# Float32r matmuls that read their moving tile from the last column to the first, in a long-convolution and feed-forward kernel

## Chip, core and metric

The kernel runs on one core of one Trainium2 chip. The metric is the device time of one execution in microseconds. Before the change it is 3116.07 us, the median of 3 runs (3114.22 to 3117.28).

## What is computed

For 4 sequences of 12480 positions and 128 channels, a filter is made from position embeddings by a small two-layer network and a decaying window, `x * v` is convolved with it along the sequence, and the result is multiplied by `x`. Each of the 49920 rows then goes through a feed-forward layer of width 2048 with a squared ReLU:

```python
u = x * v
y = irfft(rfft(u, 2 * S, axis=1) * rfft(h_filt, 2 * S, axis=0), 2 * S, axis=1)[:, :S]
x = (x * y).reshape(B * S, D)
h = np.maximum(x @ w_in, 0.0)
out = h * h @ w_out
```

## The kernel before

The convolution is a transform in four stages for each of the four sequences (`stage1` to `stage4`, lines 232 to 677). The stages are matmuls with tables of sines and cosines, and between them all values stay in the tile `W` in SBUF. Stage one to three use float32 matmuls. Stage four (`mm`, line 570) splits its operands in a high and a low word, `ah` and `al`, and multiplies them as float32r: for each of 56 values of `t` it calls `mm3` twice. `mm3` (lines 92 to 97) issues three matmuls into one accumulator: high weights by high moving words, low weights by high moving words, high weights by low moving words. Each of the three has its own 112 columns of weights and streams 256 columns. `out_t` (line 603) multiplies the accumulator by `x`, transposes and stores the rows to `zd` in DRAM. For the first sequence, `turn_first` (line 581) does the same for the first two values of `t` and feeds the first feed-forward tile directly.

The feed-forward takes 98 tiles of tokens (2 of 446, 50 of 512, 46 of 510 columns; `GN`, line 32), and each tile in 8 steps, 784 steps in all. In a step `m_h` (line 785) issues 2 x 3 matmuls of `zh` and `zl` against 128 x 128 weights into `A`; `m_g` and `m_l` square the ReLU of `A` and split it into `gh` and `gl`, on ScalarE and VectorE, element by element and in the same column order; `m_o` (line 823) issues 2 x 3 matmuls of `gh` and `gl` into the output accumulator, which collects all 8 steps of a tile. All of these are `mm3`. That makes 784 x 12 = 9408 float32r matmuls in the feed-forward, and 224 x 6 = 1344 in stage four. A third user of `mm3`, in the filter network, has 42.

The order of the work on each engine is written out by hand: the loop at line 871 runs the feed-forward steps, and `adv` (line 850) interleaves pieces of the transforms of sequences one to three. So the tensor engine gets matmuls of the feed-forward and of the stages alternately, until the transforms are done. From then on (the tail, from about 2650 us) only the feed-forward is left, and the tiles of every second step come from a pool of their own, `tp`, opened at line 878; all other feed-forward tiles come from `mp`.

```python
def mm3(o, L, R, first=True, last=True):
    lh, ll = L
    rh, rl = R
    nc.tensor.matmul(o, lh, rh, start=first, stop=False)
    nc.tensor.matmul(o, ll, rh, start=False, stop=False)
    nc.tensor.matmul(o, lh, rl, start=False, stop=last)
```

Of the kernel before, what the change touches and what calls it, by code (L numbers as in the profile page):

```python
# [7 lines left out]
F32 = mybir.dt.float32  # L8
# [9 lines left out]
I = 112  # L18
# [9 lines left out]
NS = NF // 2  # L28
# [10 lines left out]
TH = 4  # L39
CW = 256  # L40
NCW = DFF // CW


@with_exitstack
def hyena_moe_kernel(
# [34 lines left out]
    def pool(name, side="left", **kw):  # L80
        return tc.tile_pool(name=name, bufs=kw.pop("bufs", 2), side=side, reuse_waits="tile", **kw)

    def bank():
        return psf.tile([128, 512], F32, tag="F", name="F")

    def idle(k):

        o = pso.tile([128, 512], F32, tag="O", name="O")
        for _ in range(k):
            nc.tensor.matmul(o[:, :128], zeros, zeros, start=True, stop=True)  # L90

    def mm3(o, L, R, first=True, last=True):
        lh, ll = L
        rh, rl = R
        nc.tensor.matmul(o, lh, rh, start=first, stop=False)  # L95
        nc.tensor.matmul(o, ll, rh, start=False, stop=False)  # L96
        nc.tensor.matmul(o, lh, rl, start=False, stop=last)  # L97

    def load_weights(wp):
        raws = []  # L100
        for c in range(2 * NCW):
            raw = wp.tile([128, CW, 2], I32, tag="w", name="raw", bufs=2 * NCW)
            src = (w_in if c < NCW else w_out).bitcast(I32)[:, c % NCW * 2 * CW : (c % NCW + 1) * 2 * CW]
            nc.sync.dma_start(out=raw.rearrange("p a b -> p (a b)"), in_=src)
# [3 lines left out]
    def convert_weights(p, wp, raws, wt, chunks):  # L108
        V = nc.vector
        for c in chunks:  # L110
# [15 lines left out]
            V.tensor_tensor(out=top, in0=top, in1=sgn, op=ALU.bitwise_xor)  # L126
            wt[c] = wp.tile([128, 2, CW], F32R, tag="w", name="wt", bufs=2 * NCW)
            hi12, lo12 = wt[c][:, 0, :], wt[c][:, 1, :]
# [396 lines left out]
    def stage4(b, done, ring=None):  # L525
        ax = 3 if b else 2
        L, X, q, Y = {}, {}, {}, {}
# [19 lines left out]
        with pool("s4") as p:  # L547
# [22 lines left out]
            def mm(t):  # L570
                if t >= NP:
                    return
                hi, lo = q.pop(t)
                tb = L.pop(t)
                A = bank()
                o = A[:I, :256]
                mm3(o, (tb[:, 0, :], tb[:, 2, :]), (hi[:, 0], lo[:, 0]), last=False)
                mm3(o, (tb[:, 1, :], tb[:, 3, :]), (hi[:, 1], lo[:, 1]), first=False)
                Y[t] = A

            def turn_first(t):

                zf = p.tile([I, 2 * D], F32, tag="zf", name="zf", bufs=1)
                nc.vector.tensor_mul(
                    out=zf.rearrange("p (c b i) -> p b c i", b=4, c=2),
                    in0=Y.pop(t)[:I, :256].rearrange("p (b i c) -> p b c i", b=4, c=2),
                    in1=X.pop(t).rearrange("p (b c i) -> p b c i", b=4, c=2),
                )
                o = bank()
                for c in range(2):  # L590
                    nc.tensor.transpose(o[:, c * I : (c + 1) * I], zf[:, c * D : (c + 1) * D], ident)
                idle(2)
                return o[:, 1 : 2 * I]
# [9 lines left out]
            def out_t(t):  # L603
                if t not in Y:
                    return
                xv = X.pop(t).rearrange("p (b c i) -> p b c i", b=4, c=2)
                zt = Z[t // 2 % 2]
                nc.vector.tensor_mul(
                    out=zt[:I].rearrange("p (b t c i) -> p t b c i", b=4, t=2, c=2)[:, t % 2],
                    in0=Y.pop(t)[:I, :256].rearrange("p (b i c) -> p b c i", b=4, c=2),  # L610
                    in1=xv,
                )
                if t % 2 == 0:
                    return
                zs = p.tile([128, 4 * D], F32, tag="zs", name="zs")
                nc.vector.transpose(out=zs, in_=zt)
                for k, w in enumerate(GW):
                    dst = zpart(b, t // 2, k).rearrange("(i b w) -> i b w", i=32, b=4)
                    src = zs[32 * k : 32 * k + 32]
                    if k == 0:  # L620
                        dst = dst.rearrange("i b (t w) -> i (b t) w", t=2)
                        src = src.rearrange("p (b t w) -> p (b t) w", b=4, t=2)[:, :, 1:]
                    elif k == 3:
                        dst = dst.rearrange("i b (q w) -> i (b q) w", q=4)
                        src = src.rearrange("p (b q w) -> p (b q) w", b=4, q=4)[:, :, :16]
                    else:
                        src = src.rearrange("p (b w) -> p b w", b=4)
                    nc.sync.dma_start(out=dst, in_=src)
                done[b] = t + 1
# [10 lines left out]
            if b == 0:  # L640
# [5 lines left out]
                A = [turn_first(0)]  # L646
# [38 lines left out]
    def run(gen):  # L685
        for _ in gen:
            pass
# [56 lines left out]
    cvp = take("cvp")  # L744
    conv = [convert_weights(cvp, wp, raws, wt, range(k, 2 * NCW, 2)) for k in range(2)]
    run(stage2(True, True, "left", during_s2f))
# [13 lines left out]
    def wi(k, h, f):  # L760
        return wt[k * NCW + f // 2][:, h, f % 2 * 128 : (f % 2 + 1) * 128]

# [22 lines left out]
    def m_h(zT, f):  # L785
        A = psa.tile([128, 2, 512], F32, tag="A", name="A")
        for t in range(2):
            mm3(A[:, t, : zT[0].shape[1]], (wi(0, 0, 2 * f + t), wi(0, 1, 2 * f + t)), zT)
        return A

    def m_g(A, p, n, between, way):

        r = p.tile([128, 2, GM], F32, tag="r", name="r")[:, :, :n]
        hi = p.tile([128, 2, GM], F32R, tag="gh", name="gh")[:, :, :n]
        h = A[:, :, :n]
        nc.scalar.activation(r, h, AF.Relu)  # L799
        between()  # L800
        if way != "b":
            nc.scalar.activation(hi, r, AF.Square)  # L802
        if way == "p":
            nc.vector.scalar_tensor_tensor(out=h, in0=h, scalar=0.0, in1=r, op0=ALU.max, op1=ALU.mult)  # L804
            return p, h, hi, way
        nc.scalar.activation(r, r, AF.Square)  # L806
        return p, r, hi, way
# [15 lines left out]
    def m_o(i, f, hl):  # L823
        if f == 0:
            O[0] = bank() if tail and not nxt[0] else pso.tile([128, 512], F32, tag="O", name="O")
        o = O[0][:, : GN[i]]
        for t in range(2):
            mm3(o, (wi(1, 0, 2 * f + t), wi(1, 1, 2 * f + t)), (hl[0][:, t, :], hl[1][:, t, :]), first=(f == 0 and t == 0), last=(f == NS - 1 and t == 1))
        if f == NS - 1:
            return i, o  # L830
        return None

    def m_out(last):
        if last is not None:
            i, o = last
            ot = mp.tile([D, GM], F32, tag="ot", name="ot", bufs=1)[:, : GN[i]]
            nc.scalar.copy(ot, o)
            nc.sync.dma_start(out=out[:, GO[i] : GO[i] + GN[i]], in_=ot)
# [20 lines left out]
    def way(n):  # L859
        if not nxt[0]:  # L860
            return "b"
        if stage[0] == "s2":
            return "t" if n % 3 else "p"
        return "b" if stage[0] == "s3" else "p"

    late, pend, tail = [], [], []
    ready(0)
    zT = head
    owed = 2
    since = "s4", 0  # L870
    for i in range(NM):
        for f in range(NS):
            adv(1)
            A = m_h(zT, f)
            last = m_o(*pend.pop(0)) if len(pend) > 1 else None
            adv(2)
            if not nxt[0] and not tail:
                tail.append(ctx.enter_context(pool("tp")))
            late.append((i, f, m_g(A, tail[0] if tail and f % 2 else mp, GN[i], lambda: m_out(last), way(i * NS + f))))
            while len(late) > len(tail):  # L880
                x, y, st = late.pop(0)
                pend.append((x, y, m_l(st, False)))
            if i + 1 < NM:
                if f == (1 if i else 3):
                    ready(i + 1)
                    zi = zload(i + 1)
                if f == (4 if i else 6):
                    nzT = zsplit(zi)
            adv(3)
            n = i * NS + f  # L890
            if stage[0] != since[0]:
                since = stage[0], n + 4
            owed += EXTRA[done[1] > 0]
            if owed >= 1 and stage[0] in (("s3", "s4") if done[1] else ("s2", "s3", "s4")) and nxt[0] == 1 and n >= since[1]:
                owed -= 1
                since = stage[0], n + 3
                for k in range(1, 4):
                    adv(k)
        if i + 1 < NM:
            zT = nzT  # L900
# [116 lines left out]
```

## Time and profile before

| what | value |
|---|---|
| median of 3 runs | 3116.07 us |
| lowest and highest run | 3114.22, 3117.28 us |
| span of the profiled execution (first to last instruction) | 3112.0 us |
| TensorE (PE) busy | 3072.7 us, 99% |
| weight loads (PEld) busy | 2579.8 us, 83% |
| VectorE (DVE) busy | 2538.0 us, 82% |
| ScalarE (ACT) busy | 2419.1 us, 78% |
| GpSimd (POOL) busy | 1501.6 us, 48% |

The profile gives the span of the profiled execution, 3112.0 us; its own whole time is not given apart from that, and the median of the runs lies 4.1 us above the span. A matmul's time in the profile runs from its start to a modelled end that lies behind the start of the next matmul, so durations overlap. What a matmul costs the tensor engine is the distance from its start to the start of the next one, called spacing here.

### The profile page before, as it was taken

The numbers are of one execution on the slowest core, as the hardware profiler recorded it, in microseconds if no ns is written. First come the engines' busy times: TensorE is split into PE (matmuls) and PEld (weight loads), VectorE is DVE, ScalarE is ACT, GpSimd is POOL, SyncE is SP. The second block draws the span as 40 slices with busy tenths as digits, with TensorE's granted clock in tenths as the row PEclk, the third lists the DMA queues.
The fourth block names the chain that finished last, engine by engine and source line by source line (L and its number), as shares of the span: only waits on it lengthen the run. The fifth ranks groups of instructions, "written<-read, shape, count | busy, mean of one in ns | idle before, by whom it ended". The sixth has DMA issues, their size and how long they took to land.

```text
span 3112.0 us, 49107 instructions
## 1 busy us (share of the span) xinstructions
PE 3072.7 (99%) x16086; PEld 2579.8 (83%) x16086; DVE 2538.0 (82%) x3080; ACT 2419.1 (78%) x3130; POOL 1501.6 (48%) x1631
## 2 busy tenths in 40 slices
PE   9989999999999999999999999999999999999999
PEld 7767888888888888888888888888888888888887
DVE  7888898878877988878877898878877799777776
ACT  5556777777788777788888877787788887878787
POOL 1249765556544565546644575646644466000000
PEclk9999999999999999999999999999999999999999
DMA  5783574434200664434300375434410176100000
GB/s 184 263 294 99 137 166 137 124 111 145 67 21 15 151 161 132 130 91 127 115 15 21 80 176 144 133 92 121 124 51 14 36 168 156 33 24 24 24 26 20
DMA packets 342623, 323.11 MB, mean 104 GB/s; under 512 B 161968, under 2 KB 288800, under 8 KB 342368
## 3 DMA queue, kind: packets, MB, share of 16 engines
q1 hardware_dynamic: 313216, 272.25, 30.2%
q0 software_dynamic: 29152, 47.72, 6.4%
q8 instruction: 128, 2.10, 0.3%
q14 instruction: 127, 1.04, 0.1%
HBM read 231.78 MB, written 65.60 MB: 96 GB/s over the span
## 4 chain that ended last, share of the span: by engine, by line
PE 92%; POOL 2%; DMA 2%; DVE 2%; issue 1%; ACT 1%; SPq 0%; DVEq 0%; ACTq 0%; POOLq 0%
PE A L95 11%; PE A L97 11%; PE A L96 11%; PE O L97 9%; PE O L96 9%; PE O L95 9%; PE F L380 6%; PE F L492 6%; PE F L293 5%; PE F L97 4%; PE F L95 4%; PE F L96 4%; PE A L290 2%; PE A L291 1%; POOL W L405 1%
## 5 line engine op out<-in xcount | busy, mean ns | idle before, releaser
L799 ACT ACTIVATE r<-A 128x1024 f32<-128x1024 f32 (+2 forms) x784 | 803.8, 1025 | 420.8 <-PE A L97 407.0
L818 DVE TENSOR_TENSOR gl<-r,gh 128x1020 fp32r<-128x1020 f32 (+1 forms) x433 | 642.5, 1484 | 113.9 <-ACT r L806 80.0
L95 PE MATMUL A<-zh,wt 128*128 128x512 f32 (+2 forms) x1568 | 671.4, 428 | 0.9 <-DVE gl L818 0.9
L97 PE MATMUL A<-zl,wt 128*128 128x512 f32 (+2 forms) x1568 | 613.8, 391 | 0.0
L96 PE MATMUL A<-zh,wt 128*128 128x512 f32 (+2 forms) x1568 | 612.9, 391 | 0.0
L802 ACT ACTIVATE gh<-r 128x1024 fp32r<-128x1024 f32 (+2 forms) x461 | 486.9, 1056 | 62.8 <-PE O L96 57.2
L97 PE MATMUL O<-gl,wt 128*128 128x512 f32 (+2 forms) x1248 | 487.4, 391 | 4.2 <-DVE gl L818 4.2
L96 PE MATMUL O<-gh,wt 128*128 128x512 f32 (+2 forms) x1248 | 485.0, 389 | 0.0
L95 PE MATMUL O<-gh,wt 128*128 128x512 f32 (+2 forms) x1248 | 484.9, 389 | 0.0
L804 DVE SCALAR_TENSOR_TENSOR A<-A,r 128x1024 f32<-128x1024 f32 (+2 forms) x350 | 425.4, 1215 | 68.1 <-ACT r L799 66.5
L818 DVE TENSOR_TENSOR gl<-A,gh 128x1024 fp32r<-128x1024 f32 (+2 forms) x350 | 426.1, 1218 | 63.1 <-ACT gh L802 20.4
L806 ACT ACTIVATE r<-r 128x1020 f32<-128x1020 f32 (+1 forms) x434 | 460.3, 1061 | 12.5
L813 DVE CAST gh<-r 128x1020 fp32r<-128x1020 f32 (+1 forms) x323 | 225.6, 698 | 221.2 <-ACT r L806 152.7
L782 POOL TENSOR_TENSOR zl<-zi,zh 128x512 fp32r<-128x512 f32 (+2 forms) x97 | 126.4, 1303 | 522.4 <-ACT zh L781 506.1
L567 POOL TENSOR_TENSOR al<-W,ah 112x512 fp32r<-112x512 f32 x214 | 281.9, 1318 | 189.2 <-ACT ah L561 185.0
L501 POOL TENSOR_TENSOR W<-c 112x224 f32<-112x224 f32 x256 | 217.6, 861 | 285.7 <-ACT c L499 275.0
L97 PEld LDWEIGHTS A<-zl,wt 128*128 128x128 f32 x1568 | 294.6, 188 | 64.7
L95 PEld LDWEIGHTS A<-zh,wt 128*128 128x128 f32 x1568 | 295.5, 188 | 51.4 <-DVE gl L818 3.1
L96 PEld LDWEIGHTS A<-zh,wt 128*128 128x128 f32 x1568 | 296.2, 189 | 45.1
L417 POOL TENSOR_TENSOR W<-W,m 112x256 f32<-112x256 f32 x168 | 177.8, 1058 | 247.3 <-DVE m L415 233.1
L97 PEld LDWEIGHTS O<-gl,wt 128*128 128x128 f32 x1248 | 234.2, 188 | 54.5 <-DVE gl L818 5.9
L96 PEld LDWEIGHTS O<-gh,wt 128*128 128x128 f32 x1248 | 234.2, 188 | 50.6
(127 smaller groups left out, 5495.3 us busy)
## 6 DMA issues: line engine op xcount, KB each, us to landing
ht<-Hd SPq DMA_DIRECT2D x224, 256.0 KB
tb<-t POOLq DMA_DIRECT2D x224, 196.0 KB, 3.1
xt<-x SPq DMA_DIRECT2D x224, 112.0 KB
xt<-xs SPq DMA_DIRECT2D x96, 224.0 KB
vt<-vs SPq DMA_DIRECT2D x96, 224.0 KB
tb<-t2s SPq DMA_DIRECT2D x168, 112.0 KB
Hd<-he SPq DMA_DIRECT2D x28, 512.0 KB
zd<-zs SPq DMA_DIRECT2D x222, 64.0 KB
```

What stands on the lines that cost most here:

```text
L95: nc.tensor.matmul(o, lh, rh, start=first, stop=False)
L96: nc.tensor.matmul(o, ll, rh, start=False, stop=False)
L97: nc.tensor.matmul(o, lh, rl, start=False, stop=last)
L380: nc.tensor.matmul(U[:I, k * 256 : (k + 1) * 256], tb[:KP, k, :], a[:, k], start=True, stop=True)
L501: nc.gpsimd.tensor_sub(out=dst[:, 1], in0=c[:, :, 0:3:2], in1=c[:, :, 3:0:-2])
L567: eng.tensor_sub(out=lo, in0=w, in1=hi.bitcast(F32))
L799: nc.scalar.activation(r, h, AF.Relu)
L802: nc.scalar.activation(hi, r, AF.Square)
L804: nc.vector.scalar_tensor_tensor(out=h, in0=h, scalar=0.0, in1=r, op0=ALU.max, op1=ALU.mult)
L806: nc.scalar.activation(r, r, AF.Square)
L813: nc.vector.tensor_copy(hi, g)
L818: nc.vector.tensor_sub(out=lo, in0=g, in1=hi.bitcast(F32))
```

## The change

`mm3` gets a flag `back`. With it, the moving operands are read with a step of -1, from the last column to the first; the accumulator is written from its first column on, as before. Both feed-forward matmul groups and both stage-four calls set the flag; the filter network does not.

In the feed-forward the columns of `A` are therefore mirrored, and so are the tiles made from them, `r`, `gh` and `gl`; the second group reads these from their end, which puts the output columns back in order. In stage four the 128 x 2 columns of a word are read as one row of 256 from its end, so the accumulator comes out mirrored, and the two multiplications that read it (`turn_first` and `out_t`) read it from column 255 down to 0.

The pool of the tail, `tp`, first gets a small tile of 24 floats, 96 bytes in each partition, that nothing uses. In the built program before, the `gh` and `gl` tiles of `tp` start 128 bytes behind a multiple of 256 bytes; `zh`, `zl`, `gh` and `gl` of `mp` and all weight tiles `wt` start 224 bytes behind one. With the small tile, those of `tp` also start 224 bytes behind one. The tiles of stage four start 128 or 192 bytes behind one, before and after.

The instructions of every engine stand in the same order, in the same number, with the same operand sizes before and after; only access patterns and the addresses of the `tp` tiles differ.

```diff
+TP = 24
...
-    def mm3(o, L, R, first=True, last=True):
+    def mm3(o, L, R, first=True, last=True, back=False):
         lh, ll = L
-        rh, rl = R
+        rh, rl = (x[:, ::-1] for x in R) if back else R
         nc.tensor.matmul(o, lh, rh, start=first, stop=False)
         nc.tensor.matmul(o, ll, rh, start=False, stop=False)
         nc.tensor.matmul(o, lh, rl, start=False, stop=last)
...
                 o = A[:I, :256]
-                mm3(o, (tb[:, 0, :], tb[:, 2, :]), (hi[:, 0], lo[:, 0]), last=False)
-                mm3(o, (tb[:, 1, :], tb[:, 3, :]), (hi[:, 1], lo[:, 1]), first=False)
+                words = [[x[:, a].rearrange("p d c -> p (d c)") for x in (hi, lo)] for a in range(2)]
+                mm3(o, (tb[:, 0, :], tb[:, 2, :]), words[0], last=False, back=True)
+                mm3(o, (tb[:, 1, :], tb[:, 3, :]), words[1], first=False, back=True)
                 Y[t] = A
...
                     out=zf.rearrange("p (c b i) -> p b c i", b=4, c=2),
-                    in0=Y.pop(t)[:I, :256].rearrange("p (b i c) -> p b c i", b=4, c=2),
+                    in0=Y.pop(t)[:I, 255::-1].rearrange("p (b i c) -> p b c i", b=4, c=2),
...
                     out=zt[:I].rearrange("p (b t c i) -> p t b c i", b=4, t=2, c=2)[:, t % 2],
-                    in0=Y.pop(t)[:I, :256].rearrange("p (b i c) -> p b c i", b=4, c=2),
+                    in0=Y.pop(t)[:I, 255::-1].rearrange("p (b i c) -> p b c i", b=4, c=2),
                     in1=xv,
...
-            mm3(A[:, t, : zT[0].shape[1]], (wi(0, 0, 2 * f + t), wi(0, 1, 2 * f + t)), zT)
+            mm3(A[:, t, : zT[0].shape[1]], (wi(0, 0, 2 * f + t), wi(0, 1, 2 * f + t)), zT, back=True)
...
-            mm3(o, (wi(1, 0, 2 * f + t), wi(1, 1, 2 * f + t)), (hl[0][:, t, :], hl[1][:, t, :]), first=(f == 0 and t == 0), last=(f == NS - 1 and t == 1))
+            mm3(o, (wi(1, 0, 2 * f + t), wi(1, 1, 2 * f + t)), (hl[0][:, t, :], hl[1][:, t, :]), first=(f == 0 and t == 0), last=(f == NS - 1 and t == 1), back=True)
...
             if not nxt[0] and not tail:
                 tail.append(ctx.enter_context(pool("tp")))
+                tail[0].tile([128, TP], F32, tag="tp", name="tp", bufs=1)
```

## Rows read from the trace of the kernel before

**Rows 1.** The page: engines busy, granted TensorE clock by slices, chain that ended last.

```profile
span 3112.0 us, 49107 instructions
PE 3072.7 (99%) x16086; PEld 2579.8 (83%) x16086; DVE 2538.0 (82%) x3080; ACT 2419.1 (78%) x3130; POOL 1501.6 (48%) x1631
PEclk9999999999999999999999999999999999999999
PE 92%; POOL 2%; DMA 2%; DVE 2%; issue 1%; ACT 1%; SPq 0%; DVEq 0%; ACTq 0%; POOLq 0%
```

**Rows 2.** Busy us of each engine by stretches: stretch and length, engines, granted clock, DMA.

```profile
1000.00:1200.00 200.00, 198.79 (x1041) 168.73 (x1040) 178.81 (x208) 157.74 (x188) 108.20 (x125) 1.00 0.59 141
2800.00:3000.00 200.00, 200.00 (x876) 164.12 (x875) 146.62 (x147) 159.79 (x165) 11.64 (x9) 1.00 0.08 24
```

**Rows 3.** Who waited for whom, PE: us in total, times, longest.

```profile
PE F L380 <- DVE W L387: 7.9, 23, 2.2
PE F L380 <- ACT he L393: 5.7, 2, 3.5
PE O L97 <- DVE gl L818: 4.2, 4, 1.5
```

**Rows 4.** Groups by shape: float32r matmuls, whole span; count, busy us, mean ns.

```profile
L97 PE MATMUL A<-zl,wt 128*128 128x512 f32 x800 | 315.5, 394 | 0.0
L96 PE MATMUL A<-zh,wt 128*128 128x512 f32 x800 | 313.9, 392 | 0.0
L97 PE MATMUL O<-gl,wt 128*128 128x512 f32 x800 | 313.4, 392 | 4.2 <-DVE gl L818 4.2
L96 PE MATMUL O<-gh,wt 128*128 128x512 f32 x800 | 311.9, 390 | 0.0
L95 PE MATMUL O<-gh,wt 128*128 128x512 f32 x800 | 311.7, 390 | 0.0
L97 PE MATMUL A<-zl,wt 128*128 128x510 f32 x736 | 286.7, 390 | 0.0
L95 PE MATMUL O<-gh,wt 128*128 128x510 f32 x416 | 161.5, 388 | 0.0
L96 PE MATMUL F<-gh,wt 128*128 128x510 f32 x320 | 125.5, 392 | 0.0
L96 PE MATMUL F<-ah,tb 112*112 112x256 f32 x448 | 125.2, 280 | 0.0
```

**Rows 5.** Order of time, PE: 12 matmuls of 512 columns in a row; start, length.

```profile
1551.56 0.39 PE L95 MATMUL A<-zh,wt 128*128 128x512 f32 x1
...
1554.28 0.39 PE L95 MATMUL A<-zh,wt 128*128 128x512 f32 x1
```

**Rows 6.** Order of time, PE, tail: six of `tp`, six of `m_h`, six of `mp`.

```profile
2801.71 0.40 PE L95 MATMUL F<-gh,wt 128*128 128x510 f32 x1
2801.95 0.40 PE L96 MATMUL F<-gh,wt 128*128 128x510 f32 x1
...
2803.11 0.39 PE L95 MATMUL A<-zh,wt 128*128 128x510 f32 x1
...
2804.48 0.39 PE L95 MATMUL F<-gh,wt 128*128 128x510 f32 x1
2804.71 0.39 PE L96 MATMUL F<-gh,wt 128*128 128x510 f32 x1
...
2805.84 0.39 PE L95 MATMUL A<-zh,wt 128*128 128x510 f32 x1
```

**Rows 7.** Order of time, PE: three matmuls of stage four in a row.

```profile
381.17 0.28 PE L95 MATMUL F<-ah,tb 112*112 112x256 f32 x1
...
381.51 0.42 PE L95 MATMUL A<-zh,wt 128*128 128x446 f32 x1
```

**Rows 8.** The chain in order of time: eight float32 passes of 256 columns.

```profile
648.20 1.73 PE F L380 x8
```

**Rows 9.** Groups by shape: VectorE reading PSUM forwards, in mirrored pairs, in stage four.

```profile
L304 DVE COPY W<-F 64x448 f32<-64x448 f32 x96 | 58.2, 607 | 0.0
L305 DVE TENSOR_TENSOR W<-F,sign 56x448 f32<-56x448 f32 x96 | 60.4, 629 | 1.4
L608 DVE TENSOR_TENSOR z<-F,xt 112x256 f32<-112x256 f32 x222 | 90.5, 410 | 7.2 <-DMA xt<-x 7.2
```

## The prediction, made before the changed kernel had run

> **What bounds the kernel now.** [...] The waits of TensorE name a few microseconds each [rows 3]. What is left to gain or lose is the spacing of the matmuls themselves.
>
> The spacing comes from the order of time. Twelve matmuls of 512 columns start between 1551.56 and 1554.28 us: 2.72 / 12 = 227 ns each [rows 5]. In the tail, six that read `gh` and `gl` out of the pool `tp` take 2803.11 - 2801.71 = 1.40 us, 233 ns each, and six out of the pool `mp` take 2805.84 - 2804.48 = 1.36 us, 227 ns each [rows 6]. All of these stream 510 columns against the same weights, on the same clock; what differs is where the tiles lie. Durations follow the spacing: 389 or 390 ns long where the spacing is 227. I therefore read the spacing of a group as its mean duration less 162 ns. The feed-forward groups have means of 388 to 394 ns [rows 4], thus spacings of 226 to 232; weighted by count about 229 ns. (The first matmul of `m_h` is longer where float32 passes stand ahead of it; I give it the mean of its neighbours.) Stage four has 280 ns, so 118 ns for 256 columns; its best place has (381.51 - 381.17) / 3 = 113 ns [rows 7].
>
> [...]
>
> **The change part by part.** No instruction is added, removed or moved; the same number of columns is streamed. Four things differ.
>
> (a) *The direction of 9408 + 1344 moving reads.* No row shows a moving tile that is read downwards, so I bound its price. While a matmul streams, the weights of the next are read as well: weight loads are busy 83% of the span [rows 1], and both streams now run over their tiles at once. The `tp` rows say that the price depends on where a moving tile lies, by 6 ns of 227 [rows 6], and a likely partner in that is the weight stream. My inference is that the two get in each other's way for longer or shorter depending on how they are placed, and that turning one round changes this for every matmul. Best case from rows that exist: all feed-forward matmuls at 227 and stage four at 113 ns, which saves 9408 x 2 + 1344 x 5 = 19 + 7 = 26 us. [...] Worst case from rows of this type: every feed-forward matmul at the 233 ns of `tp`, 9408 x 4 = 38 us, and stage four 4 ns longer, 5 us, together 43 us more. Worst case of any kind: reads downwards at half rate, as the float32 passes run; 432 ns for 512 columns, so 9408 x 203 ns = 1910 us, and 1344 x 98 ns = 132 us more. I take 45 us saved, nearer to the 26 than to the 134: spacings between 225 and 234 ns are everywhere in this trace and nothing near 216 is, so a removal of the whole is out of what it shows, yet a change that reaches every matmul can do more than bring the others to the best place now.
>
> [...]
>
> (b) *The 96 bytes in `tp`.* They move the tiles of 83 tail steps, 6 matmuls each, 498 matmuls, to the offset that `mp` has. At 233 - 227 = 6 ns this is 3.0 us, if the offset matters in the new direction as it does in the old. It is inside (a).
>
> (c) *The mirrored reads of the accumulator by VectorE.* `out_t` runs 222 times at 410 ns. A mirrored PSUM read is in the trace: line 305 reads pairs from their end and takes 629 ns for 448 elements, line 304 reads them forwards in 607 [rows 9]. At most 22 ns more, so 222 x 0.022 = 4.9 us of VectorE, and by the same difference in kind nothing is to be gained. It is hidden: VectorE has 21 us of 200 free in its fullest stretch [rows 2], and `out_t` waits 7.2 us for its `x` tile [rows 9] without TensorE waiting for it. Without that cover the kernel would be 4.9 us slower. I take 0.
>
> (d) *ScalarE, VectorE and GpSimd in the feed-forward.* They work element by element on mirrored tiles; 0.
>
> The sum on TensorE is -45 us. TensorE is 92% of the chain [rows 1], so I let nine tenths come through; the rest goes into waits, first those of TensorE for `gl` [rows 3], since VectorE would rise from 178.81 of 200 to 178.81 of about 197. That is -41 us. The profiled span is 3112.0 us and would become 3071; the median lies 4.1 us above the span, and I carry that over: 3116.1 - 41 = 3075 us.
>
> **The rivals.**
>
> [...]
>
> *Direction does not matter.* [...] Then only (b) is left, 3 us: about 3113 us. For it: the same bytes are read in the same time, and the best and the common spacing differ by only 2 ns. Against it: the 6 ns of `tp`. [...]
>
> *The turned streams meet for longer: slower.* The place is every feed-forward step. The tiles and the weights now share the offset 224, and that offset is the cheap one in the present direction [rows 6]; turned round, the read starts at the other end of the tile, and what was the cheap placing can become the dear one. Every ns of mean spacing is 9.4 us, so it decides from a mean of 229 ns on; at the 233 ns of `tp` it gives 3116 + 43 = 3159 us. For it: placing mattered by 6 ns already. Against it: the unfavourable place is one offset out of several that the trace has.
>
> *Downward reads stream at half rate.* 3116 + 2042 = 5158 us. For it: matmuls at half rate exist in this trace [rows 8], and no row shows a downward moving read. Against it: VectorE's mirrored pairs cost it 22 ns of 607 and not twice the time [rows 9], though that is another engine and another memory.
>
> **How the numbers follow.** About 0.2% (6 us) is what a measurement of this kernel can tell from no change. The forecast, a gain between 15 and 70 us with 3075 us as its time, gets 0.44; its own range is 3046 to 3101. The whole overhead gone or nearly, 2990 to 3046, gets 0.14. Small gains of 6 to 15 us get 0.04. No change gets 0.15. Slower by placing gets 0.17, half rate 0.06. Faster is 0.44 + 0.14 + 0.04 = 0.62, same 0.15, slower 0.23. A range that leaves out no more than 2 in 10 drops half rate, the deepest tenth (the whole overhead taken to the end) and the upper end of the slower case: 3005 to 3150 us.
>
> **What would show it right or wrong.** Right: mean durations of the feed-forward groups down from 388 to 394 ns by some 4 to 5 ns, stage four from 280 to about 275, the six of `tp` and of `mp` spaced alike in the tail, and the stretch from 2800 to 3000 us, where nothing else runs, shortened by the same share as the rest. Line 608 should stay between 410 and 432 ns. If spacing falls but the span does not, the waits for `gl` of VectorE have taken it. If the groups keep their durations, direction does not matter; if they rise above 392 ns, the placing works against it. A clock below its upper level anywhere would make the sum wrong in another way.

## The result, and the profile after

The changed kernel takes 3153.98 us (median of 4 runs, 3151.35 to 3156.75) against 3115.39 us before (4 runs of the same series, 3114.22 to 3117.28): 38.6 us more, a ratio of 1.0123 with a 95% interval of 1.0109 to 1.0137. It is slower by 1.2%, well outside the noise, where a gain of 41 us was forecast, and it lies 4 us above the upper end of the range.

The page of the changed kernel, against [rows 1]: span, busy time by engine, granted clock by slices, chain.

```profile
span 3149.6 us, 49109 instructions
PE 3115.3 (99%) x16086; PEld 2584.6 (82%) x16086; DVE 2536.4 (81%) x3080; ACT 2417.5 (77%) x3130; POOL 1507.5 (48%) x1631
PEclk9999999999999999999999999999999999999999
PE 92%; POOL 2%; DVE 2%; DMA 2%; issue 1%; ACT 1%; SPq 0%; DVEq 0%; ACTq 0%; POOLq 0%
```

TensorE is busy 42.6 us longer, the other engines as long as before to within 6 us, and the granted clock is 9 tenths or more in every slice as before, 0.999 on the mean in both traces. The span grew by 37.6 us, nine tenths of the 42.6; the other 5.0 us came out of the idle time of TensorE, which fell from 39.3 to 34.3 us. Of that, its waits for VectorE's `W` have 3.0 us, 7.9 us in [rows 3] and now:

```profile
PE F L381 <- DVE W L388: 4.9, 22, 0.8
```

So the loss is in the matmuls themselves. (The two instructions that the span has more are semaphore records of VectorE.)

The groups by shape of the changed kernel (line, engine, operation, shapes, count; busy us, mean ns; idle time before), against [rows 4]. Line 96, 97 and 98 are 95, 96 and 97 of before.

```profile
L98 PE MATMUL A<-zl,wt 128*128 128x512 f32 x800 | 317.7, 397 | 0.0
L97 PE MATMUL A<-zh,wt 128*128 128x512 f32 x800 | 318.2, 398 | 0.0
L98 PE MATMUL O<-gl,wt 128*128 128x512 f32 x800 | 318.3, 398 | 3.9 <-DVE gl L820 3.9
L97 PE MATMUL O<-gh,wt 128*128 128x512 f32 x800 | 317.9, 397 | 0.0
L96 PE MATMUL O<-gh,wt 128*128 128x512 f32 x800 | 318.0, 397 | 0.0
L98 PE MATMUL A<-zl,wt 128*128 128x510 f32 x736 | 292.0, 397 | 0.0
L96 PE MATMUL O<-gh,wt 128*128 128x510 f32 x416 | 164.9, 396 | 0.0
L97 PE MATMUL F<-gh,wt 128*128 128x510 f32 x320 | 127.0, 397 | 0.0
L97 PE MATMUL F<-ah,tb 112*112 112x256 f32 x448 | 126.4, 282 | 0.0
L610 DVE TENSOR_TENSOR z<-F,xt 112x256 f32<-112x256 f32 x222 | 90.4, 410 | 6.3 <-DMA xt<-x 6.1 <-PE A L98 0.2
```

Every feed-forward group shown is at 396 to 398 ns, where they differed from 388 to 394. (The first matmul of `m_h`, left out here, rose from 439 to 444 and from 419 to 424 ns.) Stage four rose from 280 to 282. The order of time in the tail says the same of the spacing; six `m_h` matmuls, six `m_o` matmuls out of one pool and six out of the other, against [rows 6]:

```profile
2809.70 0.40 PE L96 MATMUL A<-zh,wt 128*128 128x510 f32 x1
...
2811.10 0.40 PE L96 MATMUL F<-gh,wt 128*128 128x510 f32 x1
...
2812.50 0.40 PE L96 MATMUL A<-zh,wt 128*128 128x510 f32 x1
...
2813.90 0.40 PE L96 MATMUL F<-gh,wt 128*128 128x510 f32 x1
...
2815.30 0.40 PE L96 MATMUL A<-zh,wt 128*128 128x510 f32 x1
```

All four groups of six take 1.40 us, 233 ns a matmul. Before, `tp` had 1.40 and `mp` 1.36.

Over the whole trace the mean distance from one start to the next (distances above 260 ns left out, which hold waits or float32 passes) went as follows; these are computed from the starts in the two traces.

```
columns, accumulator   matmuls   before    after
512, A                  2400     230.8     233.6 ns
512, O                  2400     228.1     233.6
510, A                  2208     228.2     233.5
510, O                  1248     227.2     233.4
510, O in the tail       960     229.8     233.3
```

The differences times the counts are 6.7 + 13.2 + 11.7 + 7.7 + 3.5 = 42.8 us, close to the 42.6 us of busy time. Stage four, filtered in the same way (distances above 130 ns left out), went from 117.6 to 118.5 ns.

### The profile page after: what moved, and what is told of

The parts are those of the page before. It is cut to its first block, busy times and chain, and to the rows that moved or that the text cites. A ratio compares the mean times of both kernels' runs of the same rounds, so it can differ in the third digit from the quotient of the medians.

```text
span 3149.6 us, 49109 instructions
## 1 busy us (share of the span) xinstructions
PE 3115.3 (99%) x16086; PEld 2584.6 (82%) x16086; DVE 2536.4 (81%) x3080; ACT 2417.5 (77%) x3130; POOL 1507.5 (48%) x1631
## 4 chain that ended last, share of the span: by engine, by line
PE 92%; POOL 2%; DVE 2%; DMA 2%; issue 1%; ACT 1%; SPq 0%; DVEq 0%; ACTq 0%; POOLq 0%
PE A L96 11%; PE A L97 11%; PE A L98 11%; PE O L98 9%; PE O L96 9%; PE O L97 9%; PE F L381 6%; PE F L493 5%; PE F L294 5%; PE F L96 4%; PE F L98 4%; PE F L97 4%; PE A L291 2%; POOL W L406 1%; PE A L292 1%
## 5 line engine op out<-in xcount | busy, mean ns | idle before, releaser
L96 PE MATMUL A<-zh,wt 128*128 128x512 f32 (+2 forms) x1568 | 679.6, 433 | 1.4 <-DVE gl L820 1.3
L97 PE MATMUL A<-zh,wt 128*128 128x512 f32 (+2 forms) x1568 | 622.1, 397 | 0.0
L98 PE MATMUL A<-zl,wt 128*128 128x512 f32 (+2 forms) x1568 | 621.5, 396 | 0.0
L98 PE MATMUL O<-gl,wt 128*128 128x512 f32 (+2 forms) x1248 | 495.1, 397 | 3.9 <-DVE gl L820 3.9
L96 PE MATMUL O<-gh,wt 128*128 128x512 f32 (+2 forms) x1248 | 494.7, 396 | 0.0
L97 PE MATMUL O<-gh,wt 128*128 128x512 f32 (+2 forms) x1248 | 494.7, 396 | 0.0
L815 DVE CAST gh<-r 128x1020 fp32r<-128x1020 f32 (+1 forms) x323 | 225.0, 696 | 239.9 <-ACT r L808 237.1
L502 POOL TENSOR_TENSOR W<-c 112x224 f32<-112x224 f32 x256 | 227.1, 899 | 285.4 <-ACT c L500 274.5
L96 PEld LDWEIGHTS A<-zh,wt 128*128 128x128 f32 x1568 | 295.5, 188 | 54.7 <-DVE gl L820 2.9
```

What stands on the lines that cost most here:

```text
L502: nc.gpsimd.tensor_sub(out=dst[:, 1], in0=c[:, :, 0:3:2], in1=c[:, :, 3:0:-2])
L815: nc.vector.tensor_copy(hi, g)
```

## The experiments

Theory 1, formed on the result: a downward read of a moving tile costs its own matmul a fixed price, wherever the tile lies and whatever the weight load does. (Upwards means from the first column to the last, downwards from the last to the first; a tile's place is the number of bytes by which it starts behind a multiple of 256.) Theory 2 is that of the prediction: the price comes from the placing of the moving tile against the weights that are loaded meanwhile.

**A first test needs no run.** At a few places TensorE waits before it loads the next weights, so that a whole matmul streams with no weight load beside it: 10 matmuls of 512 columns before, 9 after. One of each, first the matmul and the next weight load in order of time, then the matmul's own group row, of before:

```profile
1018.36 0.39 PE L97 MATMUL O<-gl,wt 128*128 128x512 f32 x1
...
1019.52 0.19 PEld L95 LDWEIGHTS A<-zh,wt 128*128 128x128 f32 x1 [1.20 <-DVE gl L818]
```

```profile
L97 PE MATMUL O<-gl,wt 128*128 128x512 f32 x1 | 0.4, 388 | 0.0
```

and of the changed kernel:

```profile
1023.43 0.40 PE L98 MATMUL O<-gl,wt 128*128 128x512 f32 x1
...
1024.41 0.19 PEld L96 LDWEIGHTS A<-zh,wt 128*128 128x128 f32 x1 [1.03 <-DVE gl L820]
```

```profile
L98 PE MATMUL O<-gl,wt 128*128 128x512 f32 x1 | 0.4, 397 | 0.0
```

All ten of before last 388 ns, all nine of after 397 or 398. The downward read lasts 9 to 10 ns longer with no weight load running.

**Only `m_o` downwards.** The edit:

```diff
-            mm3(o, ..., last=(f == NS - 1 and t == 1))
+            mm3(o, ..., last=(f == NS - 1 and t == 1), back=True)
```

> Of the changed kernel only the six matmuls of `m_o` read downwards; `m_h`, stage four and the pool of the tail stay as before, so the output columns come out mirrored within each tile. Theory 1 (a downward read costs its own matmul a fixed price, wherever the tile lies and whatever the weights do): the groups of O rise to the 397 ns of the changed kernel, those of A stay at 390 to 394, and the time takes the share that O had in the summed spacings, 23 of 40 us: 3115 + 23 = 3138 us. Theory 2 (the price comes from how the moving tile and the weight load of the next matmul are placed against each other): at the borders between A and O the weights and tiles pair differently, so the A groups move too, and the time is anywhere between 3115 and 3154.

Measured: 3138.98 us (4 runs), against 3114.77 for the kernel before in the same series, ratio 1.0074 (1.0059 to 1.0089). Groups by shape:

```profile
L95 PE MATMUL O<-gh,wt 128*128 128x512 f32 x800 | 317.1, 396 | 0.0
L96 PE MATMUL O<-gh,wt 128*128 128x512 f32 x800 | 319.3, 399 | 0.0
L97 PE MATMUL A<-zl,wt 128*128 128x512 f32 x800 | 314.1, 393 | 0.0
L97 PE MATMUL A<-zl,wt 128*128 128x510 f32 x736 | 287.0, 390 | 0.0
L96 PE MATMUL O<-gh,wt 128*128 128x510 f32 x416 | 165.1, 397 | 0.0
```

O is at 396 to 399 ns, where the changed kernel had 396 to 398, A where it was (393 and 390 ns against 394 and 390), and the time is what theory 1 gave to within 1 us. The price belongs to the matmul that reads downwards.

**Only stage four downwards**, with VectorE's mirrored reads and without the small tile. The edit takes `back=True` from `m_h` and `m_o`.

> Of the changed kernel only stage four reads downwards, with the mirrored reads of its accumulator by VectorE; the feed-forward and the pool of the tail stay as before. From the two traces the summed spacing of stage four's matmuls rose by 0.4 us, and VectorE's multiplication was no longer. Theory 1: 3115 to 3117 us, no change that can be measured. Rival (stage four carries part of the loss, through VectorE's mirrored reads and later accumulators): 5 us or more above 3115.

Measured: 3114.22 us (10 runs) against 3114.77, ratio 0.9996 (0.9987 to 1.0005). A group of stage four, one of the feed-forward and VectorE's multiplication:

```profile
L97 PE MATMUL F<-ah,tb 112*112 112x256 f32 x448 | 126.1, 282 | 0.0
L98 PE MATMUL A<-zl,wt 128*128 128x512 f32 x800 | 314.3, 393 | 0.0
L610 DVE TENSOR_TENSOR z<-F,xt 112x256 f32<-112x256 f32 x222 | 90.6, 411 | 6.7 <-DMA xt<-x 6.7
```

Stage four and VectorE carry none of the loss that can be measured: stage four's group is at 282 ns as in the changed kernel, the feed-forward's at 393 where it had 394 before, and the multiplication at 411 where it had 410.

**Only the 96 bytes in `tp`.** The edit:

```diff
                 tail.append(ctx.enter_context(pool("tp")))
+                tail[0].tile([128, 24], F32, tag="tp", name="tp", bufs=1)
```

> The kernel before with the 96 bytes in the pool of the tail and nothing else. If placing matters for upward reads, the six matmuls out of `tp` fall from 233 to 227 ns, 498 x 6 ns = 3 us: 3112 us. If the 233 ns came from something else of the tail's odd steps, 3115 us and the six stay at 233.

Measured: 3111.78 us (10 runs) against 3114.77, ratio 0.9989 (0.9980 to 0.9999). The six matmuls of either pool in the tail, in order of time:

```profile
2800.49 0.39 PE L95 MATMUL F<-gh,wt 128*128 128x510 f32 x1
...
2801.85 0.39 PE L95 MATMUL A<-zh,wt 128*128 128x510 f32 x1
...
2803.21 0.39 PE L95 MATMUL F<-gh,wt 128*128 128x510 f32 x1
...
2804.57 0.39 PE L95 MATMUL A<-zh,wt 128*128 128x510 f32 x1
```

Both sixes take 1.36 us, 227 ns a matmul, where `tp` had 1.40 us before [rows 6]. Placing is real for these upward reads. The gain in time, 3.0 us, is barely outside the noise (the interval is 0.3 to 6.2 us); of all versions that were run this one has the lowest median.

**Blocks.** Five ways of reading the 512-column tiles in turn, one a tile: `x`, `x[:, ::-1]`, and

```python
x.rearrange("p (a b) -> p a b", b=k)[:, ::-1]    # k = 2, 16, 64
```

> The kernel before, but the feed-forward tiles of 512 columns are read in five ways in turn: upwards; from the last column to the first; and in blocks of 2, 16 and 64 columns that are read from the last block to the first, upwards inside each block. m_h and m_o of a tile do the same, so the order is restored. Each way has lines of its own. Theory 1a (every downward step costs): spacing falls from 233 ns for single columns by about half for pairs (255 steps instead of 511) and nearly to the upward 226 to 229 for 16 and 64. Theory 1b (each new line of memory that is reached from above costs, whatever the order inside): pairs and, if a line is shorter than 64 bytes, blocks of 16 stay at 233, blocks of 64 fall between. Theory 1c (starting at the end of a tile costs once): all four stay at 233. Rival (any broken run costs, up or down): pairs above 233.

Measured: 3125.41 us (8 runs) against 3114.77, ratio 1.0034 (1.0024 to 1.0045). One row of each way: upwards (L96), single columns (L106), blocks of 2 (L113), of 16 (L120), of 64 (L127).

```profile
L96 PE MATMUL O<-gh,wt 128*128 128x512 f32 x160 | 62.5, 390 | 0.0
L106 PE MATMUL O<-gh,wt 128*128 128x512 f32 x160 | 63.6, 397 | 0.0
L113 PE MATMUL O<-gh,wt 128*128 128x512 f32 x160 | 63.7, 398 | 0.0
L120 PE MATMUL O<-gh,wt 128*128 128x512 f32 x160 | 63.6, 397 | 0.0
L127 PE MATMUL O<-gh,wt 128*128 128x512 f32 x160 | 62.4, 390 | 0.0
```

Single columns, pairs and 16s cost the same 397 to 398 ns; 64s cost nothing, with the 390 ns of the upward read. So neither each downward step (1a) nor the start from the end (1c) is charged. Theory 1b comes nearest, though it had the 64s between the two prices and they are at the upward one: in this run the order of pieces of 64 bytes costs 7 to 8 ns, that of pieces of 256 bytes nothing.

**Places.** The moving tiles have 64 spare columns, and tile `i` starts `SHIFT[i % 8]` columns in; every other eight tiles are read downwards.

```python
SHIFT = (0, 8, 16, 24, 32, 40, 48, 1)
x[..., k : k + GN[i]]    # k = SHIFT[i % 8]
```

> The kernel before, but the moving tiles of the feed-forward have 64 spare columns and feed-forward tile i starts 0, 8, 16, 24, 32, 40, 48 or 1 column further in (i mod 8), so 224, 0, 32, 64, 96, 128, 160 or 228 bytes behind a multiple of 256; every other eight tiles are read downwards, in lines of their own. The pool of the tail lies 128 bytes behind, plus the same shifts. Theory 1 (a downward read has its own fixed price): downwards 233 to 234 ns at every place; upwards 228 to 231 ns at 224 and 233 ns at 128, as the pool of the tail showed. Theory 2 (placing against the weights, which stay at 224): downwards the spacing differs from place to place by some 6 ns as it does upwards, and at one place at least it is below 230 ns. The time is about half of the loss of the changed kernel, 3130 to 3145 us, with what the odd place costs the other engines.

Measured: 3148.05 us (2 runs) against 3117.67 in its series, ratio 1.0097 (1.0067 to 1.0126), a little above the expected 3130 to 3145, which fits that most places are dearer than 224 upwards too. Mean spacing by place, computed from the starts (500 or so matmuls each):

```
bytes behind a multiple of 256     0     32     64     96    128    160    224    228
upwards, ns                    230.6  230.9  233.2  231.7  233.6  231.2  229.0  234.7
downwards, ns                  233.5  233.6  233.7  234.1  233.3  233.3  233.6  235.8
```

Upwards the place is worth 4.6 ns on whole 32 bytes, and the place that the kernel had, 224, is the best. Downwards it moves the spacing by 0.8 ns (233.3 to 234.1), but for tiles that start 4 bytes off (235.8). Theory 2 asked for a downward place below 230 ns; there is none. That the place does it, and not which tiles they are, can be read from the kernel before: the same eight groups of tiles, all at 224 (`tp` left out), lie at 228.4 to 228.8 ns there. The means mix tiles of 512 and of 510 columns, which differ upwards by up to 4.8 ns at one place (232.9 and 228.1 at 0), downwards by at most 1.0.

**Fewer weights.** In two tiles of four, most matmuls of `m_o` take `lhsT[:, :32]` and write 32 rows.

> The kernel before, but every other feed-forward tile is read downwards, and in two of four tiles the matmuls of m_o, but for those of the first and the last half-step, take 32 weight columns instead of 128, so that most of the output of these tiles is left out. The weight load beside such a matmul is a quarter as long. Theory 1: downwards the spacing stays at 233 ns with 32 columns as with 128; upwards it falls from 228 to the lowest that is seen, 225. Theory 2 (the weight load is the partner that costs): with 32 columns both directions fall to the same spacing, near 225 ns or below.

Measured: 3135.99 us (one run) against 3117.67. 32 weight columns upwards (L110) and downwards (L118), and 128 upwards (L95) and downwards (L102), groups by shape, with a weight load of each size.

```profile
L95 PE MATMUL O<-gh,wt 128*128 128x512 f32 x192 | 75.0, 391 | 0.0
L102 PE MATMUL O<-gh,wt 128*128 128x512 f32 x192 | 76.2, 397 | 0.0
L110 PE MATMUL O<-gh,wt 128*32 128x512 f32 x182 | 71.8, 395 | 0.0
L118 PE MATMUL O<-gh,wt 128*32 128x512 f32 x182 | 72.3, 397 | 0.0
L102 PEld LDWEIGHTS O<-gh,wt 128*128 128x128 f32 x320 | 60.1, 188 | 14.0
L118 PEld LDWEIGHTS O<-gh,wt 128*32 128x32 f32 x266 | 28.7, 108 | 20.7
```

A weight load of a quarter of the columns lasts 108 ns instead of 188, not a quarter as long as was expected. It leaves the downward price where it is, 397 ns with either, as theory 1 said. That upwards 32 columns would fall to the lowest spacing, which both theories expected, is wrong: they rise from 391 to 395 ns.

**Jumps.** Upward reads that leave blocks out and come back to them:

```python
x.rearrange("p (a t b) -> p t a b", t=2, b=k)    # m_h, k = 16, 32, 64
x.rearrange("p (t a b) -> p a t b", t=2, b=k)    # m_o
```

and blocks of 32 from the last to the first.

> As the run with blocks, but the five ways are: upwards; blocks of 32 columns from the last to the first; and three upward ways that jump: m_h reads every second block of 16, 32 or 64 columns and then the ones left out, m_o reads the columns of its mixed tiles back in order, by jumping between the two halves after each block. Nothing of the three is read downwards. Theory 1 (downwards is what costs): the jumping ways stay at the 228 to 231 ns of the upward read, blocks of 32 downwards lie at 233 as blocks of 16 do or at the upward value as blocks of 64 do. Theory 3 (what costs is that the next piece of memory isn't the one that follows, whatever the direction): jumping by blocks of 16 is at 233 to 234 ns like 16 downwards, by blocks of 64 at the upward 228 to 231, and 32 falls on the same side in both.

Measured: 3132.55 us (4 runs) against 3116.52 in its series, ratio 1.0057 (1.0037 to 1.0077). Groups by shape, `m_o`: upwards (L96), down by 32 (L110), jumping by 16 (L124), by 32 (L138), by 64 (L152).

```profile
L96 PE MATMUL O<-gh,wt 128*128 128x512 f32 x160 | 62.4, 390 | 0.0
L110 PE MATMUL O<-gh,wt 128*128 128x512 f32 x160 | 63.1, 394 | 0.0
L124 PE MATMUL O<-gh,wt 128*128 128x512 f32 x160 | 64.4, 403 | 0.0
L138 PE MATMUL O<-gh,wt 128*128 128x512 f32 x160 | 63.7, 398 | 0.0
L152 PE MATMUL O<-gh,wt 128*128 128x512 f32 x160 | 62.4, 390 | 0.0
```

Jumping upwards by 16 costs more than reading downwards, 403 against 397 ns; by 64 it is free, 390 ns, like downwards by 64. So theory 3 holds in place of theory 1: the direction is not what is charged. What is charged is that the next piece of memory isn't the one that follows, for the pieces up to 32 columns (128 bytes) that were tried, 394 to 403 ns against 390; pieces of 64 columns (256 bytes) cost nothing, 390 ns, in either of the two orders tried. Mean spacing in the runs with blocks and with jumps, computed from the starts (upwards as in the run with blocks; the run with jumps is within 0.2 ns of it):

```
512 columns, ns                  m_h     m_o
upwards                        230.5   228.8
last column to first           233.7   233.7
blocks of 2, last to first     233.7   233.8
blocks of 16, last to first    233.6   233.7
blocks of 32, last to first    231.8   232.9
blocks of 64, last to first    230.6   228.0
jumping by 16                  239.2   239.9
jumping by 32                  235.9   236.2
jumping by 64                  230.7   228.2
```

Theory 3's number for jumping by 16, 233 to 234 ns, was too low, and blocks of 32 downwards lie between the two prices. A fixed price for each break is out as well: jumping by 32 has 15 breaks and costs 5.4 to 7.4 ns, so the 7 breaks of jumping by 64 would cost some 2.5 to 3.5 ns, and they cost at most 0.3. All these tiles start at 224; sizes between 32 and 64 columns, and what in the chip sets the limit, were not tested.

**Places of the weights.** Gaps of 8 columns between the weight tiles put them at eight places, while the moving tiles stay at 224:

```diff
-            raw = wp.tile([128, CW, 2], I32, tag="w", name="raw", bufs=2 * NCW)
+            if c < NCW:
+                wp.tile([128, 8], F32, tag=f"gap{c}", name="gap", bufs=1)
+            raw = wp.tile([128, CW, 2], I32, tag=f"w{c % NCW}", name="raw", bufs=2)
```

> The kernel before, but the weight tiles of the feed-forward start 0, 32, 64, 96, 128, 160, 192 or 224 bytes behind a multiple of 256, by the step of the tile, while the moving tiles stay at 224; every other feed-forward tile is read downwards, in lines of its own. If the price of placing that the moving tiles showed upwards (229 ns at 224, 231 at 0, 233 at 64 and 128) is one against the weights, the upward spacing goes over the same values as the weights move, some 4 ns between the best and the worst place; if it belongs to the moving tile alone, it stays at 228 to 229 at all eight. Downwards 233 to 234 ns at all eight (theory 1), or the same swing as upwards (theory 2).

Measured: 3147.40 us (2 runs) against 3116.52, ratio 1.0100 (1.0070 to 1.0129). Mean spacing by the place of the weights, computed from the starts:

```
bytes behind a multiple of 256     0     32     64     96    128    160    192    224
upwards, ns                    232.4  231.4  233.1  232.5  233.2  230.3  231.0  229.8
downwards, ns                  233.4  233.5  233.5  234.7  233.8  233.7  233.5  233.6
```

Upwards the weights' place swings the spacing by 3.4 ns, so the weights do have a part in what placing costs upwards; in the kernel before, with all weights at 224 (`tp` left out), the same eight steps lie at 228.3 to 228.9 ns. Downwards it is flat to 1.3 ns.

Weights read the other way round, which would test theory 2 directly, were not run.

## Why the prediction was wrong

*What bounds the kernel* was right. TensorE stayed at 99%, the mean granted clock at 0.999, and nine tenths of what the matmuls lost came through: 37.6 of 42.6 us of span, the share that the sum had assumed for a gain.

*Part (a)*, the direction, is the step that failed, in sign. It took -45 us, with -26 as the best and +43 as the worst case from rows of the same type (and half rate beyond); the busy time of TensorE rose by 42.6. The overhead of 134 us against which the 45 was weighed is shown by no run: it takes the 216 ns of a float32 pass of 256 columns ([rows 8], 1.73 us for eight) for what 512 float32r columns could come down to, and the lowest mean spacing of 512 columns in the tables here is 228.0 (blocks of 64). The spacing that came was that of the worst row of the same type, the 233 ns of `tp`, for every feed-forward matmul. That the bound fits so well is luck as far as is known: no run shows why a downward read has the spacing of the dearest upward places (233.2 ns at 64, 233.6 at 128), and jumps go above it. The choice inside the bounds rested on an inference that no row carried: that the moving and the weight stream hinder each other and that turning one round would part them. The trace of before held a row that speaks against the size: matmuls with no weight load beside them last 388 ns, by the prediction's own reading a spacing of 226 against its mean of 229. Streams that never met would thus have saved, by an estimate from these two spacings, 3 x 9408 ns = 28 us, not 45. The runs put something else in its place. The spacing depends on the order in which the pieces of a tile are read: in pieces of 128 bytes or less that don't follow each other, downwards or by jumps, a 512-column matmul takes 232 to 240 ns instead of 228 to 231, and in pieces of 256 bytes it loses nothing (228.0 to 230.7). From the last column to the first a 512-column matmul of `m_o` lasts 397 or 398 ns with a weight load beside it or without. Why 256 bytes stays open. The prediction's own sign for a loss, groups above 392 ns, came (396 to 398), but it laid such a rise to the placing, and downwards no placing helps.

Stage four, for which the rows gave -7 to +5 us, rose by 0.9 ns a matmul, about 1 us. Its moving tiles start at 128 or 192; at 128 the feed-forward's reads cost the same both ways (233.6 and 233.3 ns), which would explain the small rise but was not tested with 256 columns.

*Part (b)*, the 96 bytes: right for upward reads (227 ns for both sixes; 3.0 us forecast, 3.0 measured alone, a closeness that is luck with an interval of 0.3 to 6.2 us). The prediction took the two sixes of [rows 6] to run against the same weights; they are of different steps and have different weights, all at 224, so it is this run that shows the place of the moving tile to be the cause. The condition attached to it, that the offset matters in the new direction as in the old, doesn't hold: downwards 128 and 224 are 233.3 and 233.6 ns. In the changed kernel the small tile gains nothing.

*Part (c)*, VectorE: right. The mean of the mirrored multiplication stayed at 410 ns, and stage four alone changed nothing that can be measured.

*The rivals.* Slower by placing, to 3159 us, came true in its time (3154) and not in its mechanism: it held the present placing to be cheap in one direction and dear in the other, while downwards every placing on whole 32 bytes is equally dear (233.3 to 234.1 ns). It had 0.17; the range, which was to leave out 2 in 10, cut it at 3150 us and missed by 4. The others are out: no mean spacing of 512 columns is near 216 ns, so the whole overhead did not go; a read from the last column to the first does cost time, 2.8 to 6.2 ns a matmul in the feed-forward; and nothing is at half rate, which from [rows 8] (216 ns for 256 columns) would be 432 ns for 512, where the highest mean is 239.9.

## What to carry to other kernels

The float32r matmuls of this kernel kept their spacing when the moving columns were read in ascending runs of 64, with the last run first or every second run first (228.0 to 230.7 ns against 228.8 to 230.5 upwards); out-of-order runs of 32 or fewer cost 1 to 11 ns of some 230. So a mirrored or permuted layout can be free if the permutation moves whole runs of 64, as far as these 512-column tiles show. Where TensorE is the bound, the places of moving tiles and weights are worth a try: moving one pool by 96 bytes was worth about 3 us here, and the other places tried for the moving tiles cost 1.6 to 4.6 ns a matmul upwards on whole 32 bytes. In the best case both stood at 224; whether it counts that they are alike was not tested. When a trace shows spread between equal matmuls, look first for those that run without the supposed partner; they tell whether the partner is one.

## What was not expected of the hardware

Jumping ahead by 16 columns costs more than going backwards by single columns: 239 to 240 ns against 233.7 for 512 columns. A read from the last column to the first loses its dependence on placing as well: the spacing is the same to 1.4 ns at every whole 32 bytes tried of moving tile and weights, while upwards it spreads over 4.6 ns. Taking three quarters of the weight columns away made upward matmuls slower, 232.1 against 228.6 ns; why stays open, as does what in the placing of an upward read costs the 4.6 ns.
